# Token halves for the queries and keys of segment 0, and each spare head's copy in two halves, with the list of work ordered anew

## The chip, the cores and the metric

The kernel runs on one core of a Trainium2 chip. What counts is the device time of one launch in microseconds (us). Five engines work side by side, each through its own list in order: TensorE (PE) multiplies matrices into PSUM, ScalarE (ACT) and VectorE (DVE) move results out of PSUM and do element-wise work, GpSimd (POOL) does masks and small things, SyncE (SP) issues transfers. ACT issues a few transfers as well.

## The reference, cut to what matters

The input is 2048 tokens of 640 features in bf16. It is a transformer block: layer norm, a segmented attention with a memory, a projection and a residual, then layer norm, a feed-forward block of 1728 with SiLU, and a residual.

```python
for s in range(4):                       # segments of 512 tokens, 32 heads of 20
    logits = q_s @ k_s^T * scale + mask  # causal inside the segment
    a_dot = softmax(logits) @ v_s
    a_mem = (phi(q_s) @ M) / (phi(q_s) @ z + 1e-6)   # phi(t) = t + 1 or exp(t)
    o_s = g * a_mem + (1 - g) * a_dot    # g = sigmoid(beta), one per head
    M, z = M + phi(k_s)^T @ v_s, z + sum(phi(k_s))
h = x + concat(o) @ wo
out = h + silu(layernorm(h) @ w1) @ w2
```

In segment 0, M and z are zero, so that a_mem is zero too.

## The kernel before, in words

The kernel is a graph of some 1,400 small tasks. Functions declare them per segment (declare_front: layer norm, values, projections, copies; declare_ticks: scores, exponentials, attention; declare_memory; declare_back: wo, second layer norm, feed-forward). A long string, ORDER, then says by hand in which order they are emitted, on which engine (a letter behind a slash: A, D, G, S), and in which buffer slot (behind a colon). Each engine's list is that string restricted to the engine. A tracker adds the semaphore waits that the reads and writes need. So nothing is scheduled at run time: an engine that waits holds up all that stands behind it in its list.

Names of tasks, for segment s and head group or chunk c:

- n1_st, n1_r, n1_ap: statistics (DVE), root (POOL), normalisation (DVE) of a token block of 128. In segment 0 it is transposed on TensorE (n1_tp) and evacuated (n1_te); later by a transposing transfer (n1_tr). n2_... is the same for the second layer norm.
- pr{s}{c}{w}: projection of chunk c, w = 0 for queries, 1 for keys, in segment 0 in token halves, x (tokens 0 to 255) and y (256 to 511). qe...: its evacuation, a cast. ex..., pha..., phb...: the exponential and the rest of phi. v..., ve...: values of a token block and their evacuation.
- qk...: the scores of a group of four heads (four small matmul strips). In segment 0 a group's scores are packed by quads: qk0x1 to qk0x3 are groups 0 to 3 in the x half, qk4x1 to qk4x3 are groups 4 to 7. e...: the exponential of the scores on ACT, for two heads (ending 0 or 2) or for four at once (+). mk...: causal mask on POOL. av, oe, tn, nm: attention times values, evacuation, transposition, division.
- kt, kg, kh, mz, ma, mb: the memory. ot, wo, rs: transposition of the attention, output projection, residual. h1, th, s: first feed-forward matmul, tanh, product. h2, o, out: second one, residual, store. w_...: loads of weights, x0, x1, x2, x4, x8, x12: loads of tokens.

**Spare heads.** The five chunks of 128 rows have four strips of 32 rows. A strip holds one head in its first 20 rows (groups 0 to 4, heads 0 to 19). The 12 rows left over take pieces of heads 20 to 31, the spare heads. For these to be used in a strip of their own (groups 5 to 7), twelve copies from SBUF to SBUF, vt{s}0 to vt{s}11 (line 914), bring the pieces from the chunks QK to the buffer QKV. In segment 0 the chunks are named QZ and QZV and lie in the buffer of w2 (w_sb), so that w2 can be loaded only when segment 0's scores are done. Group 4 needs no copy, groups 5 to 7 need all twelve:

```python
for r in range(4):
    p = 32 * r
    virt(3 * r, allq((0, 1, 2)), QKV_[p:p + 12, :, :, :], QK_[p + 20:p + 32, 0:3, :, :])
    virt(3 * r + 1, allq((3, 4)), QKV_[p + 12:p + 20, 0:2, :, :], QK_[p + 20:p + 28, 3:5, :, :])
    virt(3 * r + 2, allq((3, 4)), QKV_[p + 12:p + 20, 2, :, :], QK_[p + 28:p + 32, 3:5, :, :])
```

Each copy waits for both token halves of queries and keys of its chunks (allq), and covers, for each row, the 512 queries and the 512 keys of a chunk, which lie one behind the other. Task qk4x1 is the first that reads copied rows.

Lines: 866 and 871 are the projections (871 in parts of 128 columns), 882 and 883 their casts on ACT and DVE, 889 and 896 to 902 phi, 778 the transposes on TensorE, 790 and 791 their evacuation, 798 the transposing transfers of both layer norms, 827 and 842 values, 914 the copies, 964 the scores, 976 their exponentials, 987 the masks, 1092, 1110, 1123 and 1135 to 1137 av, oe, tn and nm of segment 0, 1264 and 1272 ot and wo, 1307 h1, 1349 h2, 578 and 581 the loads.

Of the kernel before, what the change touches and what calls it, by code (L numbers as in the profile page):

```python
# [356 lines left out]
epsg0:0 vpad0 zpad w2z/G:0 fill30:7 warm iota mt mta mtb mm7 x0:0 x1:4 mm0 n1_st1/A:0,0 w_q0:0 w_q1 w_q2 epsc sel  # L357
halfc n1_st0/D:5 n1_r0/G n1_r1/D n1_ap0:0 n1_tp0:4 n1_te0a/A:0 n1_ap1:1 n1_tp1:0 n1_te0b/A n1_te1b/D n1_te1a/A w_k0
re_wq1/D:0 pr010x:4 re_wq4/A re_wq2/D pr020x:2 qe020x/A:0 qe010x/A:0 re_wq3/D re_wq0/D pr000x:5 pr040x:6 w_k1
re_wk2/A:0 qe000x/A:0 re_wk1/D qe040x/A:0 pr011x:0 qe011x/A re_wk0/D pr001x:2 pr021x:5 qe001x/A qe021x/A x2:10,5  # L360
n1_st2/D:3 n1_r2/G qk0x10:0 pr030x:7 w_wv0:0 w_wv1 n1_st3/D:1 n1_r3/G e0x10:4 x4:2,1,11,3 qe030x/A:0 w_wo:0 beta
w_w1_0:0 e0x12 re_wk3/D pr031x:6 n1_ap2:2 re_wk4/D x8/S:6,7,8,9 n1_ap3:0 n1_tp2:0 n1_te2/D n1_st6:4 n1_tp3:4 n1_r6/G
n1_te3/A qe031x/D pr041x:7 qe041x/D qk0x20:0 e0x2+:6 pr030y:4 qe030y/D pr031y:5 qe031y/A pr041y:6 qe041y/A pr040y:7
qe040y/A vt02/S:0 vt011/S vt05/S vt08/S n1_st5:1 qk0x30:0 vt04/S mk0x1_0 mk0x1_256 n1_st4:5 n1_r5/G n1_ap5:1 e0x3+:0
n1_ap6:2 pr000y:4 qe000y/D lsc0 vt07/A pr021y:6 qe021y/D pr001y:5 qe001y/D pr011y:7 ex021:0 qe011y/D pr020y:1 n1_r4/D
mk0x3_0 qe020y/D mk0x3_256 vt010/A pr010y:6 qe010y/D vt00/A vt03/A vt06/S v03:2 ve03/D:0 ex001:1 mk0x3_384 mk0x2_0
v00:4 ve00/D qk0y10:0 e0y12:5 mk0x1_384 pha021:1 pha001:2 v01:6 e0y10 mk0y1_0 mk0x2_256 vt09/S phb021 vt01/S qk4x10:2
phb001 lsc1 n1_st7:7 e4x1+:2 vpad1 v02:0 ve01/D av0x:6 mk4x1_0 n1_ap4:3 n1_r7/G qk4x20:2 e4x2+:1 n1_tr5:0 mk4x1_256
mk4x1_384 ve02/D lsc2 lsc3 oe0x/D:0 mk4x2_0 mk4x2_256 av2x:7 ex041:1 oe2x/D:1 kt02:0 n1_tr6 mk0y1_256 mm2 kt00:1 v11:0
qk4x30:2 e4x30:3 pha011:0 ve11/D:1 tn0x:6 nm0x:3 e4x32 mk4x3_0 pha031:1 qk0ya0:0 mk4x3_256 n1_ap7:2 mk4x3_384 v12:6  # L370
e0ya+:4 w_w1_2 ve12/D av4x:4 oe4x/D:0 mz00:5 ma00/A:2,5 qk1ya0:0 e1ya2:0 tn2x:6 nm2x:0 av6x:7 oe6x/D:1 e1ya0 tn4x:6
nm4x:1 qk2ya0:2 kvz e2ya2:1 tn6x:7 mm3 nm6x:2 n1_tr4 v10:0 n1_st11:2 e2ya0 qk0y20:4 e0y2+:6 w_w1_3 w_w1_1 mk0y2_0
kg00/G:0 mk0y2_256 n1_tr7 v13:2 n1_r11/G qk3ya0:4 e3ya0:3 ve10/D n1_st9:6 n1_r9/D pha041:2 ex031:2 mm6 ve13/D ot1:0
wo1:0 n1_st8:3 e3ya2 ot0 ex011:0 wo0:2 rs1 n2_st1:0 mk0y1_384 w_w1_4 phb011 qk4ya0:4 e4ya0:2 n2_r1/D kg02/G e4ya2 rs0
n2_ap1:0 n2_st0:0 pr101:0 qe101/A:0 av0y:1 qk0y30:2 e0y3+:0 w_w2_0/S pr120:6 zf0 n2_r0/D oe0y/D:0 pr100:7 mk0y3_0
ex101:0 qk5ya0:2 n2_ap0:3 e5ya2:4 n2_tr1:0 phb041 qe100/D e5ya0 qe120/D:0 pr121:0 qe121/D qk4y10:4 mk0y3_256 tn0y:1
nm0y:3 e4y10:5 e4y12 mk0y3_384 n1_r8/D av2y:0 oe2y/D:1 qk6ya0:2 mk4y1_0 pha120:0 pr141:1 qe141/D:0 phb031 n2_tr0
h1_0_7_0:6 e6ya+:0 th0_7_0:0 s0_7_0:0 h1_0_12_0:0 th0_12_0:1 qk7ya0:1 e7ya+:1 kt01:0 w_w2_5 h1_0_4_0:7 tn2y:5 s0_12_0
h1_0_3_0:6 kg01/G mk4y1_256 n1_st10:1 th0_3_0:0 mk4y1_384 qvz h1_0_6_0:0 qk4y20:1 th0_4_0:1 nm2y:3 s0_4_0 mm4
h1_0_5_0:5 e4y2+:3 s0_3_0 pr110:7 qe110/D:0 th0_5_0:1 qk4y30:1 pr140:6 th0_6_0:0 e4y32:6 mk4y2_0 e4y30 w_w2_1/S  # L380
mk4y2_256 s0_6_0 s0_5_0 mk4y3_0 mk4y3_256 qe140/D av4y:0 kt03:1 kg03/D ex120:1 qk8a0:4 e8a0:2 e8a2 pr111:1 h1_0_1_0:2
# [75 lines left out]
""".split()  # L457


ONE_EXP = {row.partition("+")[0] for row in ORDER if row[0] == "e" and "+" in row}  # L460


def build(nc, es, A_x, A_wq, A_wk, A_wv, A_wo, A_beta, B_x, B_w1, B_w2, out):
# [471 lines left out]
    def declare_ticks(s):  # L935
# [489 lines left out]
```

## Time and profile before

| | |
|---|---|
| median of 3 runs | 298.28 us (297.99 to 299.16) |
| profiled execution | 298.33 us, its span 296.6 us |
| TensorE busy | 285.0 us, 96% of the span |
| VectorE, ScalarE, GpSimd busy | 222.8, 217.5, 139.9 us |
| DMA | 25.40 MB in 49906 packets |

The page gives each engine's busy time, and the span in 40 slices; other views list what an engine waited for, the chain of work that ended last, and the instructions in order of time. An engine is not counted as busy while it issues a transfer; such rows carry a q (SPq, ACTq). Times in them count from the start of the span.

### The profile page before, as it was taken

The page shows a single profiled execution, that of the slowest core. Times are in us where ns is not written, and L with a number is a line of the kernel's source. Part 1 is how long each engine was busy: PE and PEld are TensorE (multiplying, and loading weights), DVE is VectorE, ACT ScalarE, POOL GpSimd, SP SyncE. Part 2 cuts the span into 40 slices and gives each one's busy share as a digit, 9 for nine tenths or more (in the row PEclk, how much of TensorE's full clock was granted, in tenths as well). Part 3 has the DMA queues.
Part 4 walks back from the last instruction along what each step waited for, and adds up shares of the span by engine and source line. Part 5 has one row for each costly group of instructions (what it writes and reads, how often), then busy time and mean ns, then how long its engine had stood idle before and what let it go on. Part 6 is the DMA issues. An engine that isn't in the chain of part 4 may idle for free.

```text
span 296.6 us, 7437 instructions
## 1 busy us (share of the span) xinstructions
PE 285.0 (96%) x2991; PEld 167.6 (56%) x2991; DVE 222.8 (75%) x506; ACT 217.5 (73%) x266; POOL 139.9 (47%) x257
## 2 busy tenths in 40 slices
PE   7897879999999999999999999999999999999997
PEld 5775445545665455566643444465665457764575
DVE  3897889768989789899678967759967688626522
ACT  5875979999999899999879999788759751014400
POOL 6246834744656477646525656355576620200000
PEclk9999999999999999999999999999999999999999
DMA  7968772804943321254462400154181023220002
GB/s 208 366 209 114 192 105 68 221 18 98 168 89 75 74 39 26 37 111 66 97 140 51 77 1 2 26 75 88 20 102 32 0 59 76 68 67 25 22 22 91
DMA packets 49906, 25.40 MB, mean 86 GB/s; under 512 B 39488, under 2 KB 48032, under 8 KB 49872
## 3 DMA queue, kind: packets, MB, share of 16 engines
q1 hardware_dynamic: 48204, 23.18, 37.3%
q10 hardware_dynamic: 1668, 1.74, 1.9%
q8 instruction: 24, 0.39, 0.6%
q14 instruction: 10, 0.08, 0.1%
HBM read 10.41 MB, written 2.62 MB: 44 GB/s over the span
## 4 chain that ended last, share of the span: by engine, by line
PE 76%; DVE 8%; DMA 7%; ACT 4%; POOL 2%; issue 2%; SPq 1%; DVEq 0%; ACTq 0%
PE ps_all L1349 19%; PE ps_all L1307 15%; PE ps_all L866 12%; PE ps_all L1272 7%; PE ps_all L964 7%; PE ps_all L827 5%; PE ps_all L1008 5%; ACT PT L976 3%; DMA x_tok<-in_A_x_dram 3%; DMA xT<-xn_rot 2%; PE ps_all L1038 1%; DMA w_sb<-w_sb 1%; PE ps_all L1092 1%; PE ps_all L1225 1%; POOL PT L987 1%
## 5 line engine op out<-in xcount | busy, mean ns | idle before, releaser
L976 ACT ACTIVATE PT<-ps_all 128x1024 bf16<-128x1024 f32 (+1 forms) x120 | 153.1, 1310 | 17.7 <-PE ps_all L964 16.5
L987 POOL TENSOR_SCALAR_AFFINE_SELECT PT<-PT 128x512 bf16<-128x512 bf16 x128 | 81.5, 647 | 59.1 <-ACT PT L976 57.0
L1349 PE MATMUL ps_all<-w_sb,sT 128*128 128x320 bf16 (+2 forms) x462 | 64.9, 295 | 0.0
L1307 PE MATMUL ps_all<-hT,w_sb 128*128 128x512 bf16 (+1 forms) x325 | 63.0, 337 | 0.5 <-DVE sT L1322 0.4
L1316 ACT ACTIVATE th<-ps_all 128x512 f32<-128x512 f32 (+2 forms) x70 | 34.0, 505 | 35.1 <-PE ps_all L1307 31.0
L1349 PEld LDWEIGHTS ps_all<-w_sb,sT 128*128 128x128 bf16 x462 | 43.2, 98 | 18.3 <-issue 1.8
L1322 DVE SCALAR_TENSOR_TENSOR sT<-th,ps_all 128x512 bf16<-128x512 f32 (+2 forms) x70 | 37.8, 561 | 17.1 <-ACT th L1316 16.1
L1307 PEld LDWEIGHTS ps_all<-hT,w_sb 128*128 128x128 bf16 x325 | 29.8, 98 | 25.9 <-issue 3.2
L763 POOL TENSOR_TENSOR rst<-rst,eps_c 128x1 f32<-128x1 f32 x32 | 18.4, 579 | 25.1 <-DVE rst L757 23.5
L742 DVE BATCH_NORM_STATS2 stt<-x_tok 128x6 f32<-128x320 bf16 x62 | 27.2, 481 | 1.8 <-DMA x_tok<-in_A_x_dram 1.4
L1362 DVE SCALAR_TENSOR_TENSOR x_tok<-ps_all,x_tok 128x640 bf16<-128x640 f32 (+3 forms) x18 | 13.3, 745 | 16.7 <-PE ps_all L1349 16.6
L1070 POOL TENSOR_TENSOR otok<-on 128x320 bf16<-128x320 bf16 x24 | 19.0, 796 | 11.5 <-DVE on L1062 11.5
L1272 PE MATMUL ps_all<-wo_sb,oT 128*128 128x320 bf16 x160 | 23.8, 299 | 0.0
L883 DVE CAST QK<-ps_all 128x512 bf16<-128x512 f32 x23 | 15.7, 688 | 8.8 <-PE ps_all L866 8.7
L1062 DVE TENSOR_TENSOR on<-ps_all,rd 128x640 bf16<-128x640 f32 x24 | 19.8, 825 | 0.9
L827 PE MATMUL ps_all<-wv_sb,xT 128*128 128x320 bf16 x120 | 18.3, 299 | 1.6 <-DMA xT<-xn_rot 1.3
L1272 PEld LDWEIGHTS ps_all<-wo_sb,oT 128*128 128x128 bf16 x160 | 15.0, 98 | 7.2 <-issue 1.8
L866 PE MATMUL ps_all<-xT,wkr 128*128 128x512 bf16 x75 | 18.7, 380 | 0.0
L866 PE MATMUL ps_all<-xT,wqr 128*128 128x512 bf16 x75 | 18.2, 380 | 0.0
L842 DVE CAST Vx<-ps_all 128x640 bf16<-128x640 f32 x15 | 12.3, 819 | 5.9 <-PE ps_all L827 5.8
L1008 PE MATMUL ps_all<-PT,Vx 128*32 128x512 bf16 (+3 forms) x384 | 16.4, 301 | 0.1
L769 DVE TENSOR_SCALAR xn_rot<-x_tok,mvt,rst 128x640 bf16<-128x640 bf16 x32 | 14.8, 473 | 1.7 <-POOL rst L763 1.0
(106 smaller groups left out, 338.3 us busy)
## 6 DMA issues: line engine op xcount, KB each, us to landing
w_sb<-in_B_w_dram SPq DMA_DIRECT2D x5, 432.0 KB, 6.1
x_tok<-in_A_x_dram SPq DMA_DIRECT2D x3, 640.0 KB, 8.4
w_sb<-in_B_w_dram SPq DMA_DIRECT2D x3, 480.0 KB, 4.4
out_dram<-x_tok ACTq DMA_DIRECT2D x8, 160.0 KB, 1.8
out_dram<-x_tok SPq DMA_DIRECT2D x7, 160.0 KB, 2.0
QKV<-QK SPq DMA_DIRECT2D x12, 72.0 KB
wo_sb<-in_A_wo_dram SPq DMA_DIRECT2D x1, 800.0 KB, 10.0
sT<-in_A_wq_dram SPq DMA_DIRECT2D x2, 320.0 KB, 4.3
```

The lines of the kernel that those rows point to most:

```text
L742: T.add(DV, lambda e, hh=hh: e.bn_stats(out=stt[:, s, 6 * hh:6 * hh + 6], in_=xb[:, 320 * hh:320 * hh + 320]), reads=R((xa, xsub)), writes ...
L827: fns.append(lambda e, c=c, hh=hh: e.matmul(bank(ps, hh)[:, 0:320], lhsT=xT_[:, c, 128 * i:128 * i + 128], rhs=wv_sb[:, c, 320 * hh:320 * ...
L866: fns = [lambda e, kc=kc: e.matmul(bank(ps)[:, lo:hi], lhsT=wt[:, kc, c, :], rhs=xT_[:, kc, lo:hi], start=(kc == 0), stop=(kc == NC - 1)) ...
L964: fns.append(lambda e, j=j, o=o, r=r, q0=q0, q1=q1, qa=qa, ka=ka: e.matmul(ps_all[:, o:o + q1 - q0], lhsT=ka[32 * r:32 * r + DH, 128 * j:1 ...
L976: T.add(AC, lambda e: e.activation(out=pt[:, pta.slot, q0:q0 + nq, 0:width], in_=sc3[:, b0:b0 + nq, 0:width], func=ACT.Exp, scale=SCALE), ...
L987: T.add(PO, lambda e: e.affine_select(out=v, in_=v, pattern=[[0, 4], [1, 128]], compare_op=ALU.is_ge, fill=0.0, base=0, channel_multiplier ...
L1008: fns.append(lambda e, j=j, r=r, h=h, pa=pa, pt=pt, co=co, q0=q0, ji=ji: e.matmul(bank(po)[32 * r:32 * r + 32, q0:hi], lhsT=Vx[:, vx.slot, ...
L1272: fns.append(lambda e, c=c, hh=hh: e.matmul(bank(ps, hh)[:, 0:320], lhsT=oT[:, c, 128 * i:128 * i + 128], rhs=wo_sb[:, c, 320 * hh:320 * h ...
L1307: fns = [lambda e, c=c: e.matmul(bank(ps)[:, lo:hi], lhsT=w1_sb[:, c, 128 * f:128 * f + 128], rhs=hT[:, c, lo:hi], start=(c == 0), stop=(c ...
L1316: T.add(AC, lambda e: e.activation(out=th[:, tha.slot, lo:hi], in_=bank(ps)[:, lo:hi], func=ACT.Tanh, scale=0.5), reads=R((ps, [0])), writ ...
L1322: T.add(DV, lambda e: e.scalar_tensor_tensor(out=sT[:, f, lo:hi], in0=th[:, tha.slot, lo:hi], scalar=1.0, in1=bank(ps)[:, lo:hi], op0=ALU. ...
L1349: fns.append(lambda e, f=f, t0=t0, fr=fr, hh=hh, n=n: e.matmul(bank(pa, hh)[:, 0:n], lhsT=sT[:, f, t0:t0 + 128], rhs=w2_sb[:, fr, c0 + 320 ...
```

## The change

Queries and keys of segment 0 are laid out with the token half outside the query or key index: chunk, half, then w, then 256 tokens. A small class, ByHalf, keeps the old way of indexing. Every copy of a spare head in segment 0 becomes two, vt0nx and vt0ny, each of which waits for one half's projections and moves one half (1 KB runs instead of 2 KB). Scores of the x half wait for the x copies alone. The other segments keep their layout and their copies. The two loads of w2 that overlap a half-used chunk wait for the matching half.

```diff
+class ByHalf:
+    def __getitem__(self, key):
+        p, c, w, t = key
+        if t == slice(None):
+            return self.ap[p, c, :, w, :]
+        h = t.start // 256
...
+        return self.ap[p, c, h, w, t.start - 256 * h:t.stop - 256 * h]
...
-    QZ = w2_flat[:, 0:10 * L].rearrange("p (c w t) -> p c w t", c=5, w=2)
+    QZ = ByHalf(w2_flat[:, 0:10 * L].rearrange("p (c h w t) -> p c h w t", c=5, h=2, w=2))
...
-        WA = {0: [(qk[0], WH), (qk[1], WH), (qk[2], WH[:2])], 1: [(qk[2], WH[2:]), (qk[3], WH), (qk[4], WH[:2])],
+        H0, H1 = [(0, 0), (1, 0)], [(0, 1), (1, 1)]
+        WA = {0: [(qk[0], WH), (qk[1], WH), (qk[2], H0)], 1: [(qk[2], H1), (qk[3], WH), (qk[4], H0)],
...
-        lane_v = [T.lane(f"virt{s}a"), T.lane(f"virt{s}b")]
+        halves = ("x", "y") if s == 0 else ("",)
+        lanes_v = [[T.lane(f"virt{s}{tg}a"), T.lane(f"virt{s}{tg}b")] for tg in halves]
...
-            dma(f"vt{s}{n}", reads, [(qv, [n])], lambda e: e.dma_start(out=o, in_=i_), pr, 0.25, "sb", lane=lane_v[n % 3 > 0], engs=(SP, AC))
+            for hf, tg in enumerate(halves):
+                if s:
+                    o, i_, sub = QKV_[p0:p1, g, :, :], QK_[r0:r1, c, :, :], WH
+                else:
+                    o, i_, sub = QKV_.ap[p0:p1, g, hf, :, :], QK_.ap[r0:r1, c, hf, :, :], [(0, hf), (1, hf)]
+                dma(f"vt{s}{n}{tg}", [(qk[c_], sub) for c_ in cs], [(qv, [n + 12 * hf])],
...
-            return (qv, list(range(12))), QKV_[:, g - 5, 0, :], QKV_[:, g - 5, 1, :]
+            return (qv, list(range(24 if s == 0 and sub is WH else 12))), QKV_, g - 5
```

ORDER is written anew. Its first lines show the copies in the new place, six of them ahead of the second pair of token blocks:

```diff
-qe040y/A vt02/S:0 vt011/S vt05/S vt08/S n1_st5:1 qk0x30:0 vt04/S mk0x1_0 mk0x1_256 n1_st4:5 n1_r5/G n1_ap5:1 e0x3+:0
+qk0x10:0 e0x12:2 vt09x/S pr040x:7 qe040x/D:0 pr031x:5 pr041x:6 e0x10 mk0x1_0 mk0x1_256 mm2 qe041x/A qe031x/D vt05x/S
```

On TensorE, the stretch from the last projections of segment 0 to the first scores that read copied rows and a little on. Before (964: scores; 866: projections; 827: values; 1092: attention times values; ps_all is PSUM; w_sb holds the queries and keys):

```order
L964 MATMUL ps_all<-w_sb 128x128 x8
L866 MATMUL ps_all<-hT,wqr 128x256 x5
L866 MATMUL ps_all<-hT,wkr 128x256 x15
L866 MATMUL ps_all<-hT,wqr 128x256 x10
L827 MATMUL ps_all<-wv_sb,hT 128x320 x20
L964 MATMUL ps_all<-w_sb 128x256 x4
L964 MATMUL ps_all<-w_sb 128x128 x8
L827 MATMUL ps_all<-wv_sb,hT 128x320 x10
L964 MATMUL ps_all<-w_sb 128x256 x4
L964 MATMUL ps_all<-w_sb 128x128 x8
L827 MATMUL ps_all<-wv_sb,hT 128x320 x10
```

The third-last and second-last rows are qk4x10, which reads copied rows. Now (993: scores; 884: projections; 845: values):

```order
L993 MATMUL ps_all<-w_sb 128x256 x4
L993 MATMUL ps_all<-w_sb 128x128 x8
L845 MATMUL ps_all<-wv_sb,hT 128x320 x10
L884 MATMUL ps_all<-hT,wkr 128x256 x5
L993 MATMUL ps_all<-w_sb 128x256 x4
L993 MATMUL ps_all<-w_sb 128x128 x8
L845 MATMUL ps_all<-wv_sb,hT 128x320 x10
L993 MATMUL ps_all<-w_sb 128x256 x8
L845 MATMUL ps_all<-wv_sb,hT 128x320 x10
L993 MATMUL ps_all<-w_sb 128x256 x4
L993 MATMUL ps_all<-w_sb 128x128 x8
L884 MATMUL ps_all<-hT,wqr 128x256 x5
```

Here the fifth and sixth rows are qk4x10. Two of the three value groups that stood ahead of it (v03 and v00) and one projection (040y, the last row) now stand behind it, between the scores of the other groups.

On SP, the queue of transfers from the copies to the second layer norm's transposes. Before (914: copies; 798, 1207, 1264: transposing transfers of a normalised block, of phi of the keys, of the attention; 581 with 128x1728: a load of w1; 128x4x640 on line 581: the first load of w2):

```order
L914 DMA w_sb<-w_sb 8x2x1024
L798 DMA_TRANSPOSE xT<-xn_rot 128x5x128
L1207 DMA_TRANSPOSE phiKt<-phiK 128x4x128
L798 DMA_TRANSPOSE xT<-xn_rot 128x5x128
L1207 DMA_TRANSPOSE phiKt<-phiK 128x4x128
L581 DMA w_sb<-in_B_w_dram 128x1728
L798 DMA_TRANSPOSE xT<-xn_rot 128x5x128
L581 DMA w_sb<-in_B_w_dram 128x1728 x2
L798 DMA_TRANSPOSE xT<-xn_rot 128x5x128
L1264 DMA_TRANSPOSE oT<-otok 128x5x128 x2
L581 DMA w_sb<-in_B_w_dram 128x1728
L581 DMA w_sb<-in_B_w_dram 128x4x640
```

Now (943: copies, of 512 elements; 816, 1236, 1293: the three kinds of transposing transfers; 598: loads), from the second transposes of phi on:

```order
L816 DMA_TRANSPOSE xT<-xn_rot 128x5x128 x2
L943 DMA w_sb<-w_sb 8x2x512
L598 DMA w_sb<-in_B_w_dram 128x1728
L943 DMA w_sb<-w_sb 8x1x512 x2
L1293 DMA_TRANSPOSE oT<-otok 128x5x128
L598 DMA w_sb<-in_B_w_dram 128x1728
L1293 DMA_TRANSPOSE oT<-otok 128x5x128
L943 DMA w_sb<-w_sb 12x3x512
L943 DMA w_sb<-w_sb 8x1x512
L943 DMA w_sb<-w_sb 8x2x512 x2
L943 DMA w_sb<-w_sb 12x3x512 x2
L598 DMA w_sb<-in_B_w_dram 128x1728 x3
```

The loads of w1, of which four stood between and ahead of the transposes and one ahead of the copies, now come behind: the last three stand behind six y copies, and the transposes of the second layer norm (line 816, hT) follow them.

More of the change, by code (lines that the diff above doesn't have):

```diff
@@ L356 @@
 ORDER = """
[L357 to L361, printed above, removed]
@@ L367 @@
[L367 to L371, printed above, removed]
@@ L372 @@
[L372 to L381, printed above, removed]
@@ new lines @@
+e4x10:1 v03:0 ve03/D mk0x3_256 mk0x2_256 mm4 kt02:0 mk0y1_0 mk0y1_256 e4x12 mk4x1_0 qk4x20:2 e4x20:3 v00:6 phb001
+e4x22 qk4x30:0 e4x3+:5 pr040y:5 ve00/D vpad1 mk0x1_384 lsc2 lsc3 n1_ap4:1 qe040y/D mk0x3_384 mk4x2_0 n1_ap6:2 ex041:1
+ex011:2 v11:6 ve11/D:1 qk0ya0:2 av2x:0 av0x:1 v02:6 e0ya+:6 ve02/A oe2x/D:1 oe0x/D:0 tn0x:0 mk4x3_0 qk1ya0:2 nm0x:1
+e1ya+:2 mk4x3_256 tn2x:1 nm2x:3 mk4x2_256 mk4x1_256 mk4x1_384 mk4x3_384 av4x:6 oe4x/D:0 av6x:7 oe6x/D:1 tn4x:0 zf0
+nm4x:1 phb011 kt00:1 qk2ya0:2 vt04y/S e2ya+:0 mk0y1_384 tn6x:1 nm6x:3 n1_tr4 v10:6 kg00/D:0 mz00:1 ma00/A:1,2 qk0y20:2
@@ new lines @@
+e0y20:1 ve10/D e0y22 n1_st9:6 mk0y2_0 n1_tr6 vt010y/S w_w1_4:0 v12:0 ve12/A vt011y/S vt02y/S v13:2 n1_st11:3 qk3ya0:4
+e3ya2:3 mk0y2_256 ot0:0 wo0:0 zf1 mzc0 pha041:1 mzc7 e3ya0 ve13/D pha031:2 n1_r9/D phb031 n1_ap9:2 av0y:2 w_w1_0
+qk4ya0:3 rs0 vt08y/A pr101:7 n2_st0:7 n2_r0/D e4ya2:4 oe0y/D:1 kg02/G ot1 vt09y/S wo1:0 e4ya0 mzc3 qk0y30:2 qe101/A:0
+rs1 tn0y:6 pr100:7 n2_st1:2 n2_ap0:1 n2_r1/G nm0y:3 qe100/D vt05y/S vt07y/S pr120:1 ex101:2 n2_ap1:0 e0y3+:5 vt01y/S
+vt03y/S vt06y/S qk5ya0:2 e5ya2:2 pr121:0 qe121/D:0 mk0y3_0 mk0y3_256 mk0y3_384 e5ya0 qk4y10:4 e4y10:6 qe120/D
```

206 lines of the change are left out of this document (113 added, 93 removed).

## The prediction

> **What bounds the kernel now.** I read the page first, then the busy time by stretches, then TensorE's own waits, the chain of work that ended last, and at last the timeline of the first 60 us.
>
> ```profile
> PE 285.0 (96%) x2991; PEld 167.6 (56%) x2991; DVE 222.8 (75%) x506; ACT 217.5 (73%) x266; POOL 139.9 (47%) x257
> PE   7897879999999999999999999999999999999997
> 10.00:20.00 10.00, 9.96 (x119) 7.79 (x118) 9.46 (x32) 9.59 (x17) 4.41 (x10) 1.00 0.93 322
> 20.00:30.00 10.00, 8.45 (x96) 5.79 (x94) 7.91 (x20) 5.34 (x7) 5.70 (x11) 1.00 0.70 93
> 30.00:40.00 10.00, 8.49 (x150) 5.01 (x143) 8.62 (x20) 9.30 (x11) 8.10 (x14) 1.00 0.94 180
> 40.00:50.00 10.00, 8.69 (x110) 4.95 (x109) 9.13 (x24) 8.31 (x11) 4.48 (x10) 1.00 0.36 84
> 280.00:296.60 16.60, 14.50 (x118) 10.51 (x116) 4.62 (x8) 0.60 (x1) 0.00 (x0) 1.00 0.15 50
> ```
>
> The stretches list length, then busy time of PE, weight loads, DVE, ACT, POOL, then granted clock and DMA. TensorE is busy for 285.0 of 296.6 us at full clock. Of the 11.6 us that it is not, 2.1 lie behind the last matmuls (16.60 - 14.50), and 4.4 lie between 10 and 50 us (0.04 + 1.55 + 1.51 + 1.31): segment 0, the place of this change. That is nearly all that better order can win.
>
> ```profile
> PE ps_all L964 <- DMA w_sb<-w_sb: 1.6, 1, 1.6
> PE ps_all L827 <- DMA xT<-xn_rot: 1.3, 1, 1.3
> PE ps_all L964 <- DVE otok L1137: 0.9, 1, 0.9
> 23.86 3.78 DMA w_sb<-w_sb
> 27.77 0.43 PE ps_all L964 x12
> 35.03 7.37 DMA xT<-xn_rot
> 42.45 1.53 PE ps_all L827 x10
> ```
>
> TensorE's three longest waits behind the start-up are these, and two are in the chain: task qk4x10 waits until 27.77 for the last copy of a spare head (issued at 23.86, landed 3.78 later), and v13 until 42.45 for a transposed block that took 7.37 us from issue to landing.
>
> **The change, part by part.** The sum is made against the profiled execution (298.33 us; span 296.6, so 1.7 around it); the median of the three runs, 298.28, is the same to 0.05.
>
> *Copies.* The copies of a half need the projections of that half alone.
>
> ```profile
> 18.48 6.07 SPq L914 DMA_DIRECT2D w_sb<-w_sb  x8
> 18.49 1.63 ACTq L914 DMA_DIRECT2D w_sb<-w_sb  x1
> 20.72 3.22 ACTq L914 DMA_DIRECT2D w_sb<-w_sb  x3
> 12.23 0.40 PE L964 MATMUL ps_all<-w_sb 20*128 20x256 bf16 x12
> 12.34 0.38 ACT L882 ACTIVATE w_sb<-ps_all 128x256 bf16<-128x256 f32 x1 [0.16 <-PE ps_all L866]
> 14.78 0.72 ACT L790 ACTIVATE hT<-ps_all 128x640 bf16<-128x640 f32 x1
> 24.81 1.94 ACT L976 ACTIVATE PT<-ps_all 128x1024 bf16<-128x1024 f32 x2 [0.19 <-PE ps_all L964]
> 28.22 1.88 ACT L976 ACTIVATE PT<-ps_all 128x2048 bf16<-128x2048 f32 x1 [1.48 <-PE ps_all L964]
> 19.93 1.41 DVE L883 CAST w_sb<-ps_all 128x256 bf16<-128x256 f32 x4
> 18.82 1.80 PE L866 MATMUL ps_all<-hT,wkr 128*128 128x256 bf16 x15
> 20.45 1.25 PE L866 MATMUL ps_all<-hT,wqr 128*128 128x256 bf16 x10
> 21.54 2.88 PE L827 MATMUL ps_all<-wv_sb,hT 128*128 128x320 bf16 x20
> 24.36 0.40 PE L964 MATMUL ps_all<-w_sb 20*128 20x256 bf16 x12
> 49.46 0.40 PE L964 MATMUL ps_all<-w_sb 20*128 20x256 bf16 x12
> ```
>
> An issue on SP takes 6.07/8 = 0.76 us whether it moves 16 or 72 KB; I take 0.76 for a half too. The twelve x halves are eleven issues on SP, the y halves another eleven; one of each is ACT's. SP thus gains 22 - 8 = 14 issues, 10.6 us, and ACT loses two of its four. SP's first three x issues go at 12.9 us, when the first casts of heads 0 to 11 are done; the other eight wait for the last x casts, at 15.1, and end at 15.1 + 8 x 0.76 = 21.2. With 3.2 us to land, as the last one of before needed behind its issue (27.77 less 23.86 + 0.70 for the issue), they land at 24.4; halves have half the bytes, and two weight and token loads no longer stand ahead of them, so earlier is likelier.
>
> Who wants them: qk4x10, behind ACT's exponentials of the scores before it. I walked ACT's list from the first scores (12.4 instead of 12.2, since DVE's statistics of block 3 stand ahead of the cast qe011x). The second pair of transposed blocks is evacuated at 16.7 (before: 15.5), since DVE and ACT now take more casts ahead of it. From there ACT has two halves of an exponential (1.94), two casts (0.38 each, 0.1 of it overlapped), a whole one (1.88), two exponentials of a projection and a cast (1.4), and two halves (1.94): with the short operations 24.2. So TensorE starts qk4x10 at 24.2 instead of 27.77. But v03, v00 and projection 040y now stand behind it: two value groups at 2.82/2 = 1.4 (21.54 to 24.36) and a projection at 0.54 (three in 18.82 to 20.45), 3.3 us of the 3.6. The copies' wait is gone; net lead 0.3.
>
> *From qk4x10 to qk0y30* both orders hold the same work but for these 3.3 us. Before needed 49.46 - 27.77 = 21.7. Of it 0.9 (the row above), 0.4 (tn4x, for DVE's nm2x) and 1.3 (v13) are waits.
>
> ```profile
> 38.29 0.33 PE L1123 MATMUL ps_all<-ident,oTs 128*128 128x84 bf16 x4 [0.43 <-DVE otok L1137]
> 31.09 0.59 SPq L581 DMA_DIRECT2D w_sb<-in_B_w_dram  x1
> 33.02 1.05 SPq L581 DMA_DIRECT2D w_sb<-in_B_w_dram  x2
> 35.03 1.21 SPq L798 DMA_TRANSPOSE xT<-xn_rot  x1
> 40.24 2.90 SPq L1264 DMA_TRANSPOSE oT<-otok  x2
> 50.38 2.58 SPq L798 DMA_TRANSPOSE hT<-xn_rot  x2
> 56.84 1.26 PE L1307 MATMUL ps_all<-hT,w_sb 128*128 128x256 bf16 x10
> hT<-xn_rot SPq DMA_TRANSPOSE x16, 2.6
> x_tok<-in_A_x_dram SPq DMA_DIRECT2D x3, 640.0 KB, 8.4
> 25.20 0.48 DVE L896 TENSOR_SCALAR phiK<-w_sb 128x512 bf16<-128x512 bf16 x2
> 33.94 0.40 DVE L896 TENSOR_SCALAR phiK<-w_sb 128x512 bf16<-128x512 bf16 x1
> 78.01 2.01 PE ps_all L1349 x14
> ```
>
> The 1.3 goes: the transpose of v13 stood behind three loads of w1 issued in the 4 us ahead of it, and now all four transposes are issued before those loads. The 0.9 goes, since qk0ya0 moves ahead of av0x and tn0x and no longer waits for nm0x's bank. New by the walk are 0.3 at v00 (an exponential in two parts ends later for it), 0.55 at tn4x instead of 0.43, 0.15 at av4x, and 0.3 in small pieces: 1.3. So 2.6 - 1.3 = 1.3 won; the walk, which counts no loss of 0.1 at a handover, gives 2.4. I take 1.7. Lead at qk0y30: 0.3 + 1.7 = 2.0, from 0.3 to 2.6.
>
> *What takes it back.* The first task of the first feed-forward block (h1_0_12) needs all of w1 and the transposes n2_tr0 and n2_tr1. It could start at 56.84 - 2.0 = 54.8. But SP's queue ahead of it is longer: the first transposed attention block's issue at about 37.8 (before: 40.24), a w1 load, the second one, then six y copies (4.6 us) to 45.5, then three loads of w1 to 47.2; n2_tr0 waits for DVE to 49.3, n2_tr1 to 51.0. Landing of n2_tr1 from below: 2.6 behind its issue, 53.6, no wait. From above: as the 7.37 of the chain, also behind three such loads, 58.3. Here the loads lead by 4 us instead of 1, so I take nearer the middle, 55.9, a wait of 1.1. Behind h1_0_12 on TensorE stand h1_0_7 and qk7ya0, and ACT's e7ya+ waits for that one. Lead left: 56.84 - 55.9 = 0.9, at the ends 2.0 and -1.5.
>
> *Hidden.* The y copies land at 45.5 + 3.2 = 48.7; qk5ya0 wants them at 49.6, when e0y3+ ends; uncovered, each us late would cost one, with pr121 and qk4y10 queued behind. x8 moves on SP from ahead of the copies to behind two transposes, 25.7 by the walk; at 8.4 to land that is 34.1, and DVE's n1_st9 comes at 38 to 39. w2_0 moves behind n2_tr0 and n2_tr1, to 52, and is wanted at 78. Exponential, phi and scores of segment 0 now read two runs of 256 columns for one of 512: the same elements, so no gain; a phi takes 0.24 (0.48 for two) to 0.40, so at most 5 x 0.16 = 0.8 us on DVE, beside TensorE's work; nothing taken.
>
> *Middle and tail.* Between qk7ya0 and h1_2_7 the same work of TensorE stands ahead of each first score of a head group, with a dozen neighbours swapped; DVE gives four oT evacuations and two value evacuations to ACT, ACT gives casts and copies back. I take 0, from -0.8 to +0.8. At the end three token blocks swap places and the last block's 192 columns come before its 320; 76 matmuls of 0.14 (10 us) still cover the last normalisation: 0, ends 0.2 apart. The lead of 0.9 is then carried to the end: 298.33 - 0.9 = **297.4**.
>
> **Rivals.** *All of the lead stays* (296.3; 0.20): the w1 loads are in by 53. For it: stretch 10 to 20 moved 322 GB/s, which takes 1.3 MB in 4.1 us. Against it: 180 in 30 to 40.
>
> *The copies stay the wait* (298.3, no change; 0.20): the change doesn't do what it says. Their landing, 24.4, and the need, 24.2, differ by nothing; 2 us later eats the whole lead, one for one.
>
> *The queue of SP becomes the wait* (300.2, slower; 0.18): n2_tr1 lands 7.4 behind its issue, and up to 1.5 later where six copies hold the loads back: 58.3 to 59.8, middle 58.7, against 56.84: +1.9. It decides from a landing past 56.84, 5.8 us behind its issue; before, v13's took 7.4. For it speaks that 14 more issues stand on one queue ahead of the loads. The Trainium skill, DMA: Bandwidth & Descriptors, section Anatomy of one DMA, gives a DMA (there issued by GpSimd) a fixed 2.0 us beside bytes over 436 GB/s, so halving a 72 KB copy saves an estimated 0.08 us and the second half pays the fixed part anew. The trace agrees on the direction: 0.76 us an issue at any size; by the page alone the copies would bring no transfer time at all, only their earlier start, and this rival is the time where that costs more than it brings.
>
> **The numbers.** Forecast 0.42 (lead 0 to 1.5 at h1_0: 296.8 to 298.4), rivals 0.20, 0.20, 0.18. About 0.5% is what a measurement here can tell from no change: 296.8 and 299.8. Faster: 0.18 of the first rival, 0.13 of the forecast, 0.02 of the second: 0.33. Slower: 0.15 of the last, 0.05 of the others with a bad middle: 0.20. Rest 0.47. Range: from the walk's best lead, 2.6, with a middle better by 0.8 (294.9) to the last rival between its middle and its end (301.0).
>
> **What would show it.** In the profile after: TensorE's wait on copies gone, qk4x10 at 24 to 24.5, the chain there led by ACT exponentials; no wait on xT above 0.5; qk0y30 between 46.8 and 49; a wait of about 1 us ahead of the first 256-column w1 matmuls, released by hT<-xn_rot or the w1 loads. It is wrong if a wait on w_sb<-w_sb stays, if qk0y30 comes past 49.5, or if the middle loses over 1 us.

## The result, and the profile after

| | median | runs | against before, 95% interval |
|---|---|---|---|
| before | 298.39 us | 8 (297.38 to 299.70) | |
| changed | 299.67 us | 8 (299.02 to 300.19) | 1.0053 [1.0035, 1.0070] |

Forecast were 297.4 us and a lead of 0.9; the change costs 1.3 us by the medians and 1.6 by the ratio. The profiled execution of the changed kernel took 300.19 us (span 298.7), 1.86 more than that of before. The page gives TensorE's busy time and its 40 slices:

```profile
PE 286.2 (96%) x2997; PEld 168.9 (57%) x2997; DVE 220.1 (74%) x499; ACT 219.1 (73%) x274; POOL 141.0 (47%) x261
PE   8779899999988999999999999999999999999997
```

The 12th and 13th slice (82 to 97 us) are two 8s that before did not have. By stretches, before between 80 and 100 us (length, then PE, weight loads, DVE, ACT, POOL, clock, DMA):

```profile
80.00:90.00 10.00, 10.00 (x120) 6.20 (x120) 8.86 (x20) 9.51 (x10) 6.71 (x14) 1.00 0.51 98
90.00:100.00 10.00, 9.51 (x118) 4.99 (x115) 9.54 (x21) 8.55 (x7) 4.93 (x11) 1.00 0.32 68
```

and after:

```profile
10.00:20.00 10.00, 8.07 (x93) 6.12 (x90) 9.27 (x32) 7.97 (x18) 4.21 (x7) 1.00 0.71 234
20.00:30.00 10.00, 9.71 (x117) 6.55 (x117) 7.60 (x21) 9.95 (x15) 8.62 (x19) 1.00 0.40 51
30.00:40.00 10.00, 8.92 (x146) 5.71 (x143) 9.24 (x22) 9.17 (x8) 5.81 (x10) 1.00 0.72 172
40.00:50.00 10.00, 9.84 (x127) 6.04 (x126) 8.04 (x21) 8.00 (x12) 3.35 (x8) 1.00 0.53 129
80.00:90.00 10.00, 8.80 (x110) 5.27 (x111) 7.97 (x16) 9.43 (x10) 5.58 (x11) 1.00 0.61 71
90.00:100.00 10.00, 8.94 (x109) 4.86 (x107) 8.30 (x19) 7.13 (x8) 4.38 (x9) 1.00 0.48 92
```

From 20 to 50 us 1.26 + 0.43 + 1.15 = 2.84 us more of TensorE's time is work, more than the lead of 2.0 that was forecast for the end of this stretch. But between 10 and 20 it worked 1.89 us less than before, and between 80 and 100 1.77 less. TensorE's longest own waits after the change, behind the start-up:

```profile
PE ps_all L1067 <- DVE x_tok L1309: 1.2, 1, 1.2
PE ps_all L884 <- ACT hT L808: 1.0, 1, 1.0
PE ps_all L993 <- DMA QKV<-QK: 0.8, 1, 0.8
PE ps_all L1121 <- POOL PT L1016: 0.6, 1, 0.6
```

None is on w_sb or xT, the two that led the list before. The first is task tn8, which needs the bank that rs3 empties (and phb100's product); the second is projection 010y behind the evacuation n1_te2; the third is qk13a0, the first scores that read copied rows of segment 1, whose copies the change did not halve. The chain of work that ended last, at the two places:

```profile
3.69 6.72 DMA sT<-in_A_wk_dram
11.07 2.34 PE ps_all L884 x20
13.47 0.43 PE ps_all L993 x12
16.17 1.27 ACTq L943
17.48 0.70 ACT hT L808
```

```profile
82.96 2.64 DMA phiKt<-phiK
86.07 0.80 DVE phiK L917
86.89 0.73 DVE phiK L923
87.62 0.77 DVE phiQ L923
88.39 0.75 DVE x_tok L1309
93.19 2.79 DMA QKV<-QK
```

In the first, the last key weights (w_k1) lead, then four projections (20 matmuls), the first scores, and an issue of a copy (vt08x) by ScalarE, 1.27 us, in front of n1_te2. In the second, a transposed block of features (kt13) lands at 85.60, and behind it VectorE does pha121, phb121, phb100 and only then rs3 (lines 917, 923, 923 and 1309), at 88.31. Before, VectorE did phb100 and rs3 at these times:

```profile
79.39 0.73 DVE L902 TENSOR_TENSOR phiQ<-phiQ,ex 128x512 bf16<-128x512 bf16 x1
86.91 0.82 DVE L1280 TENSOR_TENSOR x_tok<-ps_all,x_tok 128x640 bf16<-128x640 f32 x1 [0.38 <-PE ps_all L1272]
```

And SP issued the last copies of segment 1, before (first row) and after:

```profile
90.83 1.41 SPq L914 DMA_DIRECT2D QKV<-QK  x2
92.43 2.31 SPq L943 DMA_DIRECT2D QKV<-QK  x3
```

Starts of single tasks in us, read off the timelines by the order of the tasks; the three columns on the right are runs told below, with the new order up to qk8a0 and the order of before behind it:

| | before | before again | changed | new front | and vt08x on SP | and the start |
|---|---|---|---|---|---|---|
| w_k1 landed | 9.48 | 9.87 | 10.41 | 9.89 | 9.81 | 9.70 |
| qk0x10, first scores | 12.23 | 12.30 | 13.47 | 12.95 | 12.87 | 12.09 |
| qk0x20, second scores | 15.30 | 15.60 | 16.83 | 16.31 | 16.23 | 16.01 |
| qk4x10 | 27.77 | 28.00 | 25.72 | 25.19 | 24.40 | 24.14 |
| qk0y30 | 49.46 | 48.89 | 49.20 | 48.67 | 47.87 | 47.61 |
| qk8a0 | 65.35 | 64.78 | 65.31 | 64.78 | 64.00 | 63.73 |
| tn8 | 87.95 | 87.38 | 89.18 | 87.54 | 86.76 | 86.50 |
| qk13a0 | 94.96 | 94.39 | 96.75 | 94.49 | 93.72 | 93.46 |
| last output group | 293.89 | 292.97 | 295.79 | 293.52 | 293.12 | 291.63 |

At qk8a0 the changed kernel stands level with before; at qk13a0 it is 1.79 behind, at the end 1.90.

### The profile page after: what moved, and what is told of

The parts are those of the page before. It is cut to its first block, busy times and chain, and to the rows that moved or that the text cites. A ratio compares the mean times of both kernels' runs of the same rounds, so it can differ in the third digit from the quotient of the medians.

```text
span 298.7 us, 7470 instructions
## 1 busy us (share of the span) xinstructions
PE 286.2 (96%) x2997; PEld 168.9 (57%) x2997; DVE 220.1 (74%) x499; ACT 219.1 (73%) x274; POOL 141.0 (47%) x261
## 3 DMA queue, kind: packets, MB, share of 16 engines
HBM read 10.41 MB, written 2.62 MB: 44 GB/s over the span
## 4 chain that ended last, share of the span: by engine, by line
PE 71%; ACT 12%; DVE 5%; DMA 4%; SPq 4%; issue 3%; ACTq 0%; DVEq 0%
PE ps_all L1378 18%; PE ps_all L1336 14%; PE ps_all L884 10%; ACT PT L1005 9%; PE ps_all L1301 7%; PE ps_all L993 6%; PE ps_all L845 6%; PE ps_all L1037 4%; DMA sT<-in_A_wk_dram 2%; SPq L943 2%; ACT th L1345 2%; PE ps_all L1067 2%; PE ps_all L1071 1%; PE ps_all L1254 1%; DMA QKV<-QK 1%
## 5 line engine op out<-in xcount | busy, mean ns | idle before, releaser
L1345 ACT ACTIVATE th<-ps_all 128x512 f32<-128x512 f32 (+1 forms) x70 | 34.0, 506 | 36.3 <-PE ps_all L1336 31.2
L1351 DVE SCALAR_TENSOR_TENSOR sT<-th,ps_all 128x512 bf16<-128x512 f32 (+1 forms) x70 | 38.0, 562 | 15.7 <-ACT th L1345 14.6
L1391 DVE SCALAR_TENSOR_TENSOR x_tok<-ps_all,x_tok 128x640 bf16<-128x640 f32 (+3 forms) x18 | 13.4, 745 | 18.8 <-PE ps_all L1378 18.8
L901 DVE CAST QK<-ps_all 128x512 bf16<-128x512 f32 x25 | 17.0, 687 | 6.0 <-PE ps_all L884 6.0
L778 POOL TENSOR_TENSOR rst<-mvt,eps_c 128x1 f32<-128x1 f32 x17 | 3.4, 200 | 31.4 <-DVE mvt L763 31.2
```

The source lines that it names most:

```text
L1345: T.add(AC, lambda e: e.activation(out=th[:, tha.slot, lo:hi], in_=bank(ps)[:, lo:hi], func=ACT.Tanh, scale=0.5), reads=R((ps, [0])), writ ...
L1351: T.add(DV, lambda e: e.scalar_tensor_tensor(out=sT[:, f, lo:hi], in0=th[:, tha.slot, lo:hi], scalar=1.0, in1=bank(ps)[:, lo:hi], op0=ALU. ...
```

## The experiments

My theory after the result: the loss is two waits in a row in segment 1's stage, made by the new order (rs3 late on VectorE, copies late on SP), and the front's lead was eaten at its start. The rival: the loss is spread, a price of the halves and their 12 more transfers.

**The changed kernel again.** 

> The changed kernel once more, unaltered. In its first profile the weights landed 1.0 us later than in the profile of before though they were issued at the same times and in the same order, and the first scores (qk0x10) started 1.24 us later. If that is only how transfers fell in that execution: qk0x10 at 12.4 to 12.9 this time, two stalls as in the first profile (about 1.2 us ahead of tn8 near 88 us, 0.8 us ahead of qk13a0 near 96 us), time 299.5 +- 0.4. If the new order is what makes the weights late: qk0x10 at 13.4 again.

Measured: 300.00 us, 1.0057 [1.0034, 1.0081]. The profile caught an execution of 302.38 in which a token load landed at 4.9 instead of 3.6 and TensorE's granted clock stood at 0.50 from 9.8 to 13.2 us, so it tells nothing of the start. The runs below do.

**The residual first.** On VectorE:

```diff
 pha121
-phb121
-phb100
 rs3
+phb121
+phb100
```

> On VectorE the residual add rs3 goes ahead of phb121 and phb100; all other engines as in the changed kernel. Theory of two waits in a row (a bank that rs3 frees late, then the last copies of segment 1's spare heads on SP): the 1.2 us wait ahead of tn8 goes, but the copies land as late as before, so the wait ahead of qk13a0 grows by about the same; time 299.5, within 0.3 of the changed kernel. Theory that PE's order alone counts and the copies follow PE: 1.2 us less, 298.4. Theory that the loss is spread (halves, more DMA): 299.6 and the stall shows up elsewhere.

Measured: 300.18 us, 1.0058 [1.0039, 1.0077], no gain. TensorE's timeline:

```profile
89.14 0.32 PE L1067 MATMUL ps_all<-Mzb,phiQ 128*128 128x84 bf16 x4 [1.03 <-DVE phiQ L923]
96.94 0.40 PE L993 MATMUL ps_all<-QKV 20*128 20x512 bf16 x4 [1.07 <-DMA QKV<-QK]
```

The time stayed at that of the changed kernel (300.00 in the run above), as expected, but not for the reason: tn8 waits nearly as long, now for phb100 itself, whose phi(q) it multiplies. The edit moved the wrong one of two, and the time does not part the theories, since a spread loss would have given the same.

**The copies first.** On SP:

```diff
+vt19
+vt16
 kt04
...
-vt19
-vt16
...
+vt18
+vt14
 kt13
-vt18
...
-vt14
-out0
 n1_tr8
 vt110
 vt10
 vt11
+out0
```

> On SP four copies of segment 1's spare heads move ahead of two transposes of feature blocks (kt04, kt13) and the first output store behind the last copy; all other engines as in the changed kernel. Two waits in a row: the wait ahead of qk13a0 (0.84) goes, that ahead of tn8 (1.2) stays; time 298.8, 0.8 less than the changed kernel. Theory that the loss is spread: 299.6.

Measured: 299.34 us, 1.0038 [1.0008, 1.0067]. The time is 0.5 above the forecast, the gain against the changed kernel, 0.7 (300.00 in the run above), is close to the 0.8 forecast. The wait at qk13a0 is gone in its trace; tn8 waits 1.80.

**Both.** 

> Both edits together. Two waits in a row: both go, qk13a0 starts within 0.4 us of where it did in the kernel before, less whatever lead stands at 60 us; time 297.8 (297.4 to 298.2), 1.8 less than the changed kernel and no slower than the kernel before. Theory that the loss is spread: 299.4 or more, with other waits in the place of these two.

Measured: 299.22 us, 1.0031 [1.0007, 1.0055], a miss, and near the 299.4 of the rival. tn8 still waits 1.10 for phb100, so only one of the two waits was mended.

**Before again.** 

> The kernel before, unaltered, for a second profile of its start. In four of the five profiles of the changed kernel's start that are not disturbed, the first scores (qk0x10) began at 13.0 to 13.6 us, in the one profile of before at 12.23; its last key weights (w_k1) landed at 9.5, theirs at 9.9 to 10.5. If the new order makes the start late: 12.2 to 12.5 again. If it is how the loads fall: 12.8 to 13.6, with w_k1 at 9.9 or later. Time 298.3, ratio 1.

Measured: 298.03 us, 1.0003 [0.9984, 1.0022]; the first scores at 12.30 with w_k1 at 9.87. The new front had them at 12.95 with w_k1 at 9.89. So the new order makes the first scores 0.65 later at the same landing. The landing itself scatters by more, between 9.5 and 11.4 over all the profiles, though the issue stands at 3.7 in each. A second thing shows here, on TensorE, at v13:

```profile
40.96 0.40 PE L964 MATMUL ps_all<-w_sb 20*128 20x256 bf16 x8
41.34 1.52 PE L827 MATMUL ps_all<-wv_sb,xT 128*128 128x320 bf16 x10
```

v13 starts without a wait. Its transposed block landed 5.9 us behind its issue, not 7.4: the wait of 1.31 that the prediction booked as won is not there in every execution of before.

**phb100 into idle time, and the copies.** On VectorE phb100 goes ahead of pha121, phb121 behind rs3; SP as above.

> As the run with both edits, but phb100 is moved on VectorE ahead of pha121 (into an idle 0.9 us) rather than behind rs3, since the run showed tn8 waiting for phb100's product (phiQ) itself, and phb121 goes behind rs3. If the two waits in a row are the loss: tn8 without a wait, qk13a0 at most 0.3 us after where it stood in before by the same start, time 298.2 (297.8 to 298.6), 1.0 less than the run with both edits, 1.6 less than the changed kernel. If the loss is spread over the middle: 299.2 as that run.

Measured: 299.10 us, 1.0026 [1.0004, 1.0049]; executions from 297.81 to 300.17.

```profile
87.94 0.33 PE L1067 MATMUL ps_all<-Mzb,phiQ 128*128 128x84 bf16 x4
95.51 0.40 PE L993 MATMUL ps_all<-QKV 20*128 20x512 bf16 x4 [0.85 <-DMA QKV<-QK]
```

The time is the one that the rival gave (299.2), so it does not speak for the two waits; the trace does. tn8 no longer waits. TensorE, 1.2 us sooner there than in the changed kernel, then waits for the copies, which SP issues no sooner. The two waits are in a row: mending one hands its time to the other.

**The new front alone.** ORDER of the changed kernel up to qk8a0, then what is left in the order of before; a few buffer slots differ.

> Halves and the new order up to the task qk8a0 (65 us), then the order of before to the end. If all of the loss lies in the middle (65 us on): 298.3 (298.0 to 298.7), no wait above 0.5 us between 66 and 100 us, qk8a0 at 65.3 as in both profiles. If the halves or the front cost time that shows only later: 299.3 or more.

Measured: 298.31 us, 1.0001 [0.9984, 1.0018]. So the loss of the changed kernel lies behind 65 us. And the front, halves and all, is worth nothing against before: at the same landing of w_k1 it is 0.22 ahead at qk0y30 (48.67 against 48.89) and level at qk8a0.

**The new rest alone.** Halves, the order of before up to qk8a0 with both halves of a copy one behind the other, then the new order.

> Halves in the layout, but the order of before up to qk8a0, both halves of a spare head copied one behind the other at the place of the whole copy, then the new order. If the loss lies in the middle and SP's 12 more issues in the front are what they were sized at (0.76 us each, uncovered): the last copy for qk4x10 lands about 8 us later in SP's list of eight, 4 us of them uncovered; qk4x10 at 32 instead of 27.8, and behind it the two waits of the middle, 1.5 to 1.9: 303 to 304. If halves go at the speed of wholes (two issues for the price of one): 300.

Measured: 304.59 us, 1.0213 [1.0186, 1.0239]. SP's timeline, and TensorE's waits:

```profile
17.63 12.90 SPq L943 DMA_DIRECT2D w_sb<-w_sb  x16
```

```profile
PE ps_all L993 <- DMA w_sb<-w_sb: 4.2, 1, 4.2
```

The time is 0.6 above the forecast range. A half costs 12.90/16 = 0.81 us of SP, as much as a whole. The halves without an order that splits them put qk4x10 at 31.24, 3.2 to 3.5 us behind before, and qk0y30 at 54.05, 4.6 to 5.2 behind. Part of that second figure is the clock: behind the wait for the copies it stood at 0.50 for 3.4 us, and ten matmuls of a value group took 2.85 us there, 1.53 just ahead of the wait. The stretch of 2 us inside it (PE, weight loads, DVE, ACT, POOL, clock, DMA):

```profile
32.00:34.00 2.00, 2.00 (x9) 1.19 (x8) 0.00 (x0) 1.73 (x1) 0.20 (x1) 0.50 0.77 119
```

The new front earns all this back and no more.

**vt08x on SP** (in the run with the new front alone). `vt08x/A` becomes `vt08x/S`, behind vt02x.

> The run with the new front and the order of before behind it (298.3), and one edit: the x half of the copy vt08 is issued by SP behind the eleven others and not by ScalarE, where its issue took 1.27 us ahead of the evacuation n1_te2. If ScalarE's chain sets qk4x10: the 1.0 us wait ahead of pr010y goes, qk4x10 comes 0.7 to 1.2 us sooner behind the first scores than in that run (12.24 there, 11.1 to 11.5 here), time 297.5. If the landing of the copies sets it (the last issue 0.7 us later): 12.5 to 13 behind the first scores with a wait on w_sb, time 298.5.

Measured: 297.50 us, 0.9979 [0.9953, 1.0005]. On TensorE, projection 010y in the new front alone, and here:

```profile
17.71 0.72 PE L884 MATMUL ps_all<-hT,wqr 128*128 128x256 bf16 x5 [1.00 <-ACT hT L808]
```

```profile
16.91 0.72 PE L884 MATMUL ps_all<-hT,wqr 128*128 128x256 bf16 x5 [0.29 <-ACT hT L808]
```

qk4x10 comes 0.79 sooner and the end keeps it: the time is 0.8 below the run that it edits (0.7 by the ratios to before). ScalarE's list set the pace, not the copies' landing, though the last of them is now issued later. The Trainium skill, Trainium Kernel Development and Optimization (section Key Constraints), says that issuing from several engines saves only the sequencer's issue time; here that is the whole matter, with the sign turned: the issue cost ScalarE 1.25 us where ScalarE was short of time and SP was not.

**The start in the manner of before.** The order of the first projections on TensorE, and the engine of one copy into SBUF behind them (shown in part; the casts of 011x and 021x and the copies re_wq2 and re_wq3 swap ScalarE and VectorE too):

```diff
-pr000x pr010x pr030x pr021x pr001x pr011x pr020x qk0x10
+pr000x pr010x pr020x pr011x pr001x pr021x qk0x10 pr030x
-re_wk4/A
+re_wk4/D
```

> The run with the new front and the order of before behind it, with the start put back in the manner of before: the projections 011x, 001x, 021x directly ahead of the first scores and 030x behind them, re_wk1 and re_wk0 first, re_wk4 on VectorE. The first scores came 3.06 to 3.11 us behind the landing of w_k1 in six profiles with the new start and 2.3 to 2.75 in three with the old. If the order of the start costs this: 2.4 here, and 0.6 of lead, of which the end keeps 0.3 to 0.6: 297.8. If VectorE's longer list (0.5 us more ahead of the statistics) takes it back: qk0x20 as late as before behind the landing, 298.3.

 

> Both edits of the front together, order of before behind it. If ScalarE's chain and the start both bind: a lead of 1.2 to 1.7 at qk0y30 against the kernel before, of which the wait for n2_tr1 (landed 1.0 us ahead of its use in the changed kernel) takes back up to 0.5: 297.2 (296.6 to 297.8), faster than the kernel before. If the copies' landing binds: 298.2.

Measured: 299.88 us (1.0058 [1.0037, 1.0080]), and with vt08x on SP 298.65 (1.0004 [0.9986, 1.0023]). Both worse than what they edit:

```profile
13.32 0.40 PE L993 MATMUL ps_all<-w_sb 20*128 20x256 bf16 x12 [0.97 <-DVE w_sb L901]
```

The swap had put 021x in a bank that the scores need, and its cast stands on VectorE behind statistics of 1.1 us. In the profile of the first run the granted clock also stood at 0.50 for 3.4 us from 19.4 us, so that not all of its loss is this wait. The experiment missed: it did not test the start.

**Three copies and the bank.** As the run with phb100 moved, and vt10 ahead of kt04 on SP too.

> The changed kernel with the bank freed early and the copies first, as the run before the last group, and one more copy of segment 1 (vt10) ahead of kt04 on SP: the copies' last issue 0.8 us sooner. If the two waits are all that the middle loses: no wait over 0.2 us ahead of tn8 and of qk13a0, qk13a0 within 0.1 us of the kernel before by the same qk8a0, time 298.3 (297.9 to 298.7), 0.8 less than with two edits. If something else holds the middle: 299.0.

Measured: 298.03 us, 0.9989 [0.9964, 1.0014]: level with before, as expected of the two waits. But the executions lie in two groups, eight at 297.05 to 298.13, four at 299.23 to 299.42, and the profile caught one of the four. Its chain, and VectorE:

```profile
83.95 4.03 DMA phiKt<-phiK
```

```profile
88.01 0.30 DVE L917 TENSOR_SCALAR phiK<-QK 128x512 bf16<-128x512 bf16 x1 [2.08 <-DMA phiKt<-phiK]
```

kt13 landed 4.0 us behind its issue instead of 2.4, pha121 waited for it, and rs3 stood behind pha121.

**The residual ahead of that wait.** rs3 ahead of pha121; then the same with vt08x on SP.

> As the run before the last group with the middle mended, and rs3 goes ahead of pha121 as well, which waits for the transposed block kt13. In the profile of that run (299.42, one of four executions near 299.3, the other eight lay at 297.1 to 298.1) kt13 landed 4.0 us behind its issue, at 87.99, pha121 and rs3 stood behind it, and tn8 waited 1.3; in the run with two edits it landed after 2.4. If the landing of kt13 behind rs3's place is what parts the executions: all of them at 297.2 to 298.3 here, median 297.8, no wait ahead of tn8. If they part for another reason: the slower group at 299.3 stays.

 

> The same, and the x half of vt08 issued by SP and not by ScalarE. The edit gave 0.8 us in the run with the order of before behind it (297.5 against 298.3). If the gains of front and middle add: 297.0 (296.6 to 297.4), faster than the kernel before. If the lead is lost at n2_tr1 or in the longer list of SP: 297.8 as without it.

Measured: 299.11 us (1.0028 [1.0007, 1.0049]; 298.15 to 300.65), and 297.61 (0.9975 [0.9957, 0.9993]). The first is a miss: no two groups any more, but no gain either, though its one profile (298.30) shows neither wait, only 0.53 at wo2 for nm8. The second lies between its two forecasts, and it is level with the run that has the same front and the old order behind it (0.9979): with vt08x on SP, too, the mended middle costs no more than the old one. In its profile kt13 again took 4.0. VectorE and TensorE there:

```profile
87.04 0.29 DVE L917 TENSOR_SCALAR phiK<-QK 128x512 bf16<-128x512 bf16 x1 [0.53 <-DMA phiKt<-phiK]
```

```profile
86.72 0.33 PE L1067 MATMUL ps_all<-Mzb,phiQ 128*128 128x84 bf16 x4
90.42 1.52 PE L1301 MATMUL ps_all<-wo_sb,oT 128*128 128x320 bf16 x10 [0.98 <-DVE on L1091]
```

tn8 is free of kt13, but nm8 now stands behind it on VectorE, and wo2 waits 0.98 for nm8. A late block holds up whatever is next in that list. That the slower executions of the first run are of this kind is not shown; why its median lies 1.1 above that of the run before stays open.

**The start with banks to match.** In the run with vt08x on SP: order of projections as in the diff above, 021x in a bank of its own, casts of 011x and 001x on ScalarE, re_wk4 behind them.

> The run with the issue of vt08 on SP and the order of before behind the front (297.5), with the start in the manner of before once more: projections 011x, 001x, 021x directly ahead of the first scores, casts of 011x and 001x first on ScalarE and re_wk4 behind them, but 021x in a bank that the scores do not need (in the start run above they waited 1.0 us for its cast, which stood behind statistics on VectorE). If the order of the start costs 0.6: first scores 2.4 to 2.6 us behind the landing of w_k1, 297.0. If VectorE's statistics ahead of the second scores (qk0x20) set the pace: first scores early but qk0x20 as before, 6.4 us behind the landing of w_k1, 297.5.

Measured: 297.29 us, 0.9960 [0.9944, 0.9975], the fastest of all, 0.4% below before. TensorE, first and second scores:

```profile
12.09 0.40 PE L993 MATMUL ps_all<-w_sb 20*128 20x256 bf16 x12
16.01 0.40 PE L993 MATMUL ps_all<-w_sb 20*128 20x256 bf16 x8 [0.21 <-DVE hT L809]
```

The first scores start 2.39 us behind w_k1 (3.06 before the edit), the second 6.31 (6.42 before it; 5.7 to 5.8 in the old kernel). The time lies between the two forecasts; the trace is the rival's: VectorE's statistics and the evacuation behind them set the second scores, and of the 0.67 that the first scores gain behind the landing only 0.11 is left at the second, 0.26 at qk4x10 (24.14 against 24.40, with w_k1 0.11 sooner).

## Why the prediction was wrong

**Right.** The copies' wait is gone; an issue on SP costs the same for a half; from qk4x10 to qk0y30 the changed kernel took 23.48 us where the sum had 47.5 - 24.2 = 23.3; no wait above 0.5 on xT is left; the tail cost next to nothing (1.90 behind at the last output group, 1.89 at qk31a0, the last task of scores). The prediction's "0.76 us whether it moves 16 or 72 KB" is only a mean: in that row a 16 KB copy took 0.64 to 0.65 (0.83 the first) and a 72 KB copy 0.78 to 0.80. A half took as long as its whole, so the sum of the issues held.

**"Middle and tail ... I take 0, from -0.8 to +0.8."** This is the step that failed, and it turns the sign. It counted TensorE's work ahead of each first score and found it the same. The waits came from the other lists, of which it says only that "a dozen neighbours" swap and that evacuations, casts and copies change engine: phb100 8 us later, rs3 behind it, an output store and a transpose ahead of the last three copies. The middle lost 1.8 us, at these two places; "if the middle loses over 1 us" was one of the prediction's own signs of being wrong. Against the forecast of 297.4 the profiled execution is 2.8 longer: 1.9 is this step, 0.9 the lead that should have been there at 65 us and was not.

That the loss lies behind 65 us is shown by the run with the new front alone. That it is these two waits rests on the traces and on two runs: the one with both mended (298.03), and the one with vt08x on SP as well (297.61). From qk8a0 to qk13a0 TensorE took 29.61 us in both profiles of before, 31.4 in the changed kernel, 29.85 in the run with both mended and rs3 ahead of pha121, and 30.86 and 30.30 in the two profiles where kt13 took 4.0. Against it stands the median of 299.11 of that one run, which is not explained.

**"First scores 12.4", "evacuated at 16.7".** They came at 13.47 and 18.18. Of the 1.07 by which the first is off, 0.93 is the later landing of w_k1 in that execution and the rest the order of the start (0.65 behind before, when both landed at 9.9; 0.2 was allowed for). The second is off by this 1.07 and by 0.41 more. There vt08x's issue on ScalarE was not counted at all: I gave ScalarE a gain for issuing two copies where it had issued four, and overlooked that one of the two moved from idle time to the place directly ahead of n1_te2. It is worth 0.8 us (297.50 against 298.31). So qk4x10 came at 25.72, not at 24.2. From n1_te2's end to it the sum has 7.5 and the profile 7.54, though the pieces that the prediction lists for it add to 7.8.

**"The 1.3 goes."** It went, but in a second profile of before it is not there. A stall behind a transfer was booked at the size that one execution showed; with 0 to 1.3, the middle is half. In the profile that the sum was made from it was won, and the late qk4x10 (1.5) and 0.2 behind it bring the lead of 2.0 at qk0y30 down to the 0.26 of the table; against the second profile of before 0.22 is left.

**"What takes it back", 1.1.** It did not happen. n2_tr1 landed at 55.85 where 55.9 was forecast, but that is luck: it was issued at 53.28, not 51.0, and took 2.57 to land, not 4.9. TensorE came to h1_0_12 only 1.05 behind the landing. In the run with the most lead it is the same: n2_tr1 landed at 54.26, issued at 51.69, and TensorE came at 55.31. The rival built on this, SP's queue in front of w1, had the right sign for the wrong place, and its 300.2 is near the 299.67 by luck: SP's list did become a wait, but at segment 1's copies.

## What to carry to other kernels

When a whole order is written anew, price every list, not the critical engine's alone: for each wait of that engine that was at zero before, ask what now stands ahead of its releaser. An issue of a transfer is work of the engine that issues it, and the same issue is dear or free by whose list it stands in, and ahead of what. A stall behind a transfer that one profile shows is a sample: give it a range down to nothing before booking it as a gain.

## What the runs showed of the hardware that was not expected

Two transposes issued directly one behind the other on SP, kt13 and n1_tr11, landed in one of two ways: 2.4 to 2.5 and 4.3 to 5.2 us behind their issues (four runs: the copies first, both, phb100 moved, rs3 ahead of pha121), or 4.0 and 3.2 to 3.3 (two runs), in kernels whose lists differ little there.

The first copy that ScalarE issues was dear, wherever it stood: 1.53 to 1.63 us in the two profiles of before (at 18.5 to 18.8 us) and 1.62 in the run with the new rest alone, 1.25 to 1.53 for vt08x in the ten profiles where it is the first. Later copies in the same lists took 0.64 to 0.90. The y half vt08y took 0.65 behind vt08x, but 1.27 to 1.36 in the four runs where vt08x is on SP and vt08y became the first. So that edit did not save ScalarE the dear issue; it moved it from 16 us to 43 us, where it cost less.

In three profiles the granted clock stood at 0.50 for 3.4 us: from 9.8 (the changed kernel again), 31.3 (the new rest alone) and 19.4 us (the start in the manner of before). In the 3.4 us ahead TensorE had been idle for 1.7, 3.3 and 1.7 us. The new front alone has a stretch of 3.4 us with as much idle time, 1.7, and no such drop, so what sets it off is not shown.
